# A fused attention and gated feed-forward kernel: its instruction order written out task by task, with a softmax chain in finer steps

## The chip, the cores and the metric

The kernel runs on one core of a Trainium2 chip. The metric is the device time of one execution in microseconds. In the profile, PE is the matrix engine and PEld its weight loads, DVE the vector engine, ACT the scalar engine, POOL the GpSimd engine and SP the engine that here only issues transfers. Times inside a profile count from the start of its span, which leaves out a little of the device time.

## The reference

Four batches of 6336 rows and 256 columns go through an attention over columns and then, row by row, through a gated layer.

```python
def _attn_ref(q, k, v, tau):                      # q, k, v: (4, 6336, 256)
    qn = q / (np.linalg.norm(q, axis=1, keepdims=True) + 1e-06)
    kn = k / (np.linalg.norm(k, axis=1, keepdims=True) + 1e-06)
    s = kn.transpose(0, 2, 1) @ qn / tau          # 256 x 256 in each batch
    s = s - s.max(-1, keepdims=True)
    a = np.exp(s)
    a /= a.sum(-1, keepdims=True) + 1e-09
    return (v @ a).astype(np.float32)

def _moe_ref(x, w_h, w_t, b_t):                   # x: (25344, 256)
    H = np.maximum(x @ w_h, 0.0)
    T = 1.0 / (1.0 + np.exp(-(x @ w_t + b_t)))
    return (T * H + (1.0 - T) * x).astype(np.float32)
```

## The kernel before

Each batch passes three parts.

- **Stage 1** reads q and k, 128 rows at a time (50 steps in a batch, called s), and sums the products of k with q, and of k and q with themselves for the norms, in two accumulators of the matrix engine.
- **The chain** turns the sums into the softmax matrix and folds the two weights into it (tiles mr0 and mr1).
- **Stage 2** takes 256 rows of v at a time (25 groups in a batch, 100 in all, called g): it transposes them (tr, and ev, the copy out), multiplies them by three matrices (h, t and x), applies relu (r) and gate (g) on ACT, and forms the product (p) and the result (y) on DVE. An output chunk is stored when its four groups are done.

Stage 1 of batch b+1 runs beside stage 2 of batch b. The stage 1 step, and the squares of q, which for the first 40 steps of batches 1 to 3 are taken from the matrix engine and given to ACT and POOL:

```python
for c in range(2):                                # in one step of stage 1
    nc.tensor.matmul(sg[c][:, 0:C], kc, qa, start=first, stop=False)
    nc.tensor.matmul(sg[c][:, C : C + P], kc, kc, start=False, stop=False)
    if not apart(b, s // CH):                     # b > 0 and chunk < 5
        nc.tensor.matmul(sg[c][:, C + P : C + 2 * P], qa[:, cs], qa[:, cs], ...)

def squares(b, j, half):                          # 128 x 1024 elements
    nc.scalar.activation(out=sq, in_=qa, func=Act.Square)

def sum_squares(b, j, step):                      # all on POOL
    if step == 0:   add(out=sq, in0=sq, in1=other)                       # 1024 wide
    elif step == 1: add(out=sq[:, 0:2, :], in0=sq[:, 0:2, :], in1=sq[:, 2:4, :])
    else:           ...                           # twice 256 wide
```

The chain, cut:

```python
dq = dve(lambda: (diagonal(0), diagonal(1), rest_of_q()), ...)   # norms of q
nq = pool(lambda: norm(0), ...)                   # square root
dk = dve(lambda: (diagonal(2), diagonal(3)), ...) # norms of k
nk = pool(lambda: norm(2), ...)
gs = act(copy_g, 0.58, 0.7, [dk], drop=own)       # both accumulators copied out
iq = dve(lambda: (recip(0), dcat()), ...)         # dcat: identity x 1/norm, 128 x 256
cqb = pe(bcast, 0.43, [iq], take=["vt"])          # ones @ dcat: 1/norm of q on all rows
# then scale, exp, transpose, copy, fold with the weights, and
def evac_ah(c, e):                                # 512 wide, one engine
    o, a, r = mr_t[b][c][:, C : 3 * C], st["ah", c], st["ri"][:, c : c + 1]
```

The order in which the instructions are emitted, which each engine then keeps, is chosen while the program is built. A small model of engines, buffers and transfers runs, and whenever an engine is free it takes the ready task with the lowest key:

```python
PRIO = {"tr": (24.974, 16.445, 34.195, 63.304), "ev": (74.59, ...), ...}

def pick(e):
    quiet = held(self.sums_stop)                  # no squares while a chain runs
    best = min((x for x in avail[e] if ready(x) and not (quiet and x.soft >= quiet)),
               key=lambda x: (x.key, x.n), default=None)
    lst = in_order.get(e)                         # loads and stores, in a fixed order
    if best is None and lst and ready(lst[-1]) and not (e == "POOL" and held(self.loads_stop)):
        return lst[-1]                            # no loads while a chain starts
    return best
```

Loads are issued by POOL and turn f32 into f16 on the way. Stores are issued by SP. To give loads the way, a store is put behind a later output tile by a small transfer called hold (held_row, 1 KB). In the last batch three and a quarter chunks of v are transposed by transfers (vT) and the rest by the matrix engine.

Of the kernel before, what the change touches and what calls it, by code (L numbers as in the profile page):

```python
# [15 lines left out]
P = 128  # L16
# [6 lines left out]
AHEAD = 16  # L23
BY_DMA = 3
SHORT = 1.08
MOVE = 165e3
APART = 5
V_AHEAD = 2


PRIO = {
    "tr": (24.974, 16.445, 34.195, 63.304),
    "ev": (74.59, 73.008, 67.512, 50.704),
    "h": (-53.39, -86.015, -64.208, -14.641),
    "bias": (-28.394, 23.065, -1.772, 4.453),
    "t": (4.111, -1.918, 67.766, 74.312),
    "relu": (46.555, -20.175, -1.498, 14.915),
    "x": (0.958, -19.433, 43.343, -6.4),
    "gate": (-54.132, 37.28, -94.231, -112.222),
    "prod": (-40.861, -10.819, -26.763, -55.482),  # L40
    "res": (53.604, 18.42, 116.457, -9.113),
    "s1": (117.419, 42.459, 84.45),
    "sq": (-15.195, 72.384, 19.395),
}
POW = 0.75
HEAD = 5.5
TAIL = 66
EV = BIAS = ("ACT", "DVE")
ENDS = [18, 48.5, 62.25]


class Ring:


    def __init__(self, bufs):
        self.bufs = bufs
        self.freed = []

    def open_at(self, t):
        n = len(self.freed) - self.bufs  # L60
        return n < 0 or (self.freed[n] is not None and self.freed[n] <= t)


class Task:
# [3 lines left out]

    def __init__(self, eng, key, pitch, lat, deps, fn, take=(), drop=(), size=0, follows=()):
        self.eng, self.key, self.pitch, self.lat = eng, key, pitch, lat
        self.deps, self.fn, self.take, self.drop, self.size = deps, fn, take, drop, size
        self.follows = follows
        self.start = self.done = None
        self.late = 0.0
        self.soft = 0
        self.held = {}
        self.serial = False

    def engines(self):
        return self.eng if isinstance(self.eng, tuple) else (self.eng,)

    def settle(self, e):
        n = self.eng.index(e)
        self.pitch, self.lat = self.pitch[n], self.lat[n]
        self.fn = partial(self.fn, e)
        self.eng = e


class Plan:

# [8 lines left out]
    def __init__(self):  # L101
        self.tasks = []
        self.rings = {}

        self.loads_stop, self.sums_stop = [], []

    def ring(self, tag, bufs):
        self.rings[tag] = Ring(bufs)

    def add(self, *args, **kw):  # L110
        t = Task(*args, **kw)
        self.tasks.append(t)
        return t

    def run(self):
        queues = {"POOL": [], "SP": []}
        in_order = {"POOL": [], "SP": []}
        users, followers = {}, {}
        for n, x in enumerate(self.tasks):
            x.n, x.left, x.at = n, len(x.deps) + len(x.follows), 0.0  # L120
            for d in x.deps:
                users.setdefault(d, []).append(x)
            for d in x.follows:
                followers.setdefault(d, []).append(x)
            if x.size or x.serial:
                in_order[x.eng].append(x)
        for lst in in_order.values():
            lst.sort(key=lambda x: (x.key, x.n), reverse=True)
        engines = list(dict.fromkeys(x.eng for x in self.tasks if not isinstance(x.eng, tuple)))
        avail = {e: [x for x in self.tasks if e in x.engines() and not x.left and not (x.size or x.serial)] for e in engines}  # L130
        free = dict.fromkeys(engines, 2.1)
        lanes, order, events = [], [], [0.0, 2.1]
        t, left = 0.0, len(self.tasks)
        eps = 1e-6

        def ready(x):
            return (
                not x.left
                and x.at <= t + eps
                and all(self.rings[g].open_at(t + eps) for g in x.take)  # L140
                and (x.eng != "POOL" or not x.size or sum(d > t + eps for d in lanes) < self.LANES)
            )

        def finish(x, when):
            x.done = when
            events.append(when)
            for owner, tag in x.drop:
                self.rings[tag].freed[owner.held[tag]] = when
            release(users.get(x, ()), when)

        def release(us, when):
            for u in us:
                u.left -= 1
                u.at = max(u.at, when)
                if not u.left and not (u.size or u.serial):
                    for e in u.engines():
                        avail[e].append(u)

        def pick(e):
            quiet = held(self.sums_stop)  # L160
            best = min(
                (x for x in avail[e] if ready(x) and not (quiet and x.soft >= quiet)),
                key=lambda x: (x.key, x.n), default=None,
            )
            lst = in_order.get(e)
            if best is None and lst and ready(lst[-1]) and not (e == "POOL" and held(self.loads_stop)):
                return lst[-1]
            return best

        def held(stops):  # L170
            return next(
                (
                    n + 1 for n, (a, b) in enumerate(stops)
                    if a.start is not None and (b.done is None or b.done > t + eps)
                ),
                0,
            )

        while left or any(queues.values()):
            for e in engines:  # L180
                x = pick(e) if free[e] <= t + eps else None
                if x is None:
                    continue
                if x.size or x.serial:
                    in_order[e].pop()
                else:
                    for other in x.engines():
                        avail[other].remove(x)
                    if isinstance(x.eng, tuple):
                        x.settle(e)  # L190
                left -= 1
                x.start = t
                order.append(x)
                for g in x.take:
                    x.held[g] = len(self.rings[g].freed)
                    self.rings[g].freed.append(None)
                free[e] = t + x.pitch
                release(followers.get(x, ()), free[e])
                events.append(max(free[e], t + 2 * eps))
                if x.size:  # L200
                    queues[e].append([x, float(x.size), t + self.HEAD])
                    events.append(t + self.HEAD)
                    if e == "POOL":
                        x.lane = len(lanes)
                        lanes.append(1e9)
                else:
                    finish(x, t + x.lat)

            act = [qq for qq in queues.values() if qq and qq[0][2] <= t + eps]
            share = self.RATE / max(1, len(act))  # L210
            nxt = [x for x in events if x > t + eps] + [t + qq[0][1] / share for qq in act]
            assert nxt, "no task can start"
            nxt = min(nxt)
            for qq in act:
                qq[0][1] -= share * (nxt - t)
            t = nxt
            events = [x for x in events if x > t - eps]
            for qq in act:
                if qq[0][1] < 1.0:
                    x = qq.pop(0)[0]  # L220
                    finish(x, t + self.LAG + x.late)
                    if x.eng == "POOL":
                        lanes[x.lane] = t + self.LAG
        self.end = max(x.done for x in order)
        return order
# [3 lines left out]
def kernel(  # L229
# [37 lines left out]
        "sq": 2, "vT": 3, "vT_t": 1, "o": O_BUFS, "ot": 1, "uu": 3, "pp": 3, "vtsb": 9, "mr0": 2, "mr1": 2,  # L267
        "sg0": 1, "sg1": 1, "vt": 1, "t": 1, "h": 2, "d": 2,
# [73 lines left out]
    def plan_load(nm, b, j, s=0, n=CH):  # L342

        size = P * n * C * 4 if j < NJ else TR * 2 * C * 4
        tag = nm if j < NJ else f"tail_{nm}"
        x = plan.add(
            "POOL", len(plan.tasks), 0.54, 0, [], lambda: load(nm, b, j, s, n),
            take=[tag] if s == 0 else [], size=size * (1 if j < NJ and n > 2 else SHORT),
        )
        ld.setdefault((nm, b, j), []).append(x)  # L350
        x.first = s
# [43 lines left out]
    plan_load("v", 0, 0)  # L395


    ends = [(-1, HEAD)] + [(e, (n + 1) * NS) for n, e in enumerate(ENDS)]

    def slot_of(n):  # L400

# [693 lines left out]
```

## Time and profile before

| what | value |
|---|---|
| device time, median of 3 runs | 270.34 us (270.19 to 270.39) |
| span of the profile | 268.3 us |
| PE, ACT, DVE, POOL busy | 246.4, 195.1, 181.6, 131.7 us |
| read from HBM, written to it | 78.38 MB, 25.95 MB |
| moved by the transfers, as received | 67.24 MB |

The profile page gives the busy time of each engine, the span in 40 slices, the chain of work that ended last and the costliest groups of instructions. In the page a matmul's end is modelled, so starts are the firmer reading. Transferred bytes count as they arrive: a load of f32 that lands as f16 counts half of what it reads.

### The profile page before, as it was taken

The numbers are of one execution on the slowest core, as the hardware profiler recorded it, in microseconds if no ns is written. First come the engines' busy times: TensorE is split into PE (matmuls) and PEld (weight loads), VectorE is DVE, ScalarE is ACT, GpSimd is POOL, SyncE is SP. The second block draws the span as 40 slices with busy tenths as digits, with TensorE's granted clock in tenths as the row PEclk, the third lists the DMA queues.
The fourth block names the chain that finished last, engine by engine and source line by source line (L and its number), as shares of the span: only waits on it lengthen the run. The fifth ranks groups of instructions, "written<-read, shape, count | busy, mean of one in ns | idle before, by whom it ended". The sixth has DMA issues, their size and how long they took to land.

```text
span 268.3 us, 6249 instructions
## 1 busy us (share of the span) xinstructions
PE 246.4 (92%) x2430; PEld 216.6 (81%) x2430; DVE 181.6 (68%) x377; ACT 195.1 (73%) x365; POOL 131.7 (49%) x167
## 2 busy tenths in 40 slices
PE   0697977999999999999999999999999999999991
PEld 0596864889989978999999878999998778888880
DVE  1000035777766789557878797586878998998994
ACT  1001016978888789999898887787798999998980
POOL 7233468688778064695689138567655110000000
PEclk9999999999999999999999999999999999999998
DMA  6999999999999999999999999999999999999995
GB/s 107 215 211 208 206 206 202 212 213 214 214 213 212 213 214 255 247 263 269 275 286 258 267 267 254 249 236 281 287 280 239 284 214 304 379 399 165 351 423 232
DMA packets 24622, 67.24 MB, mean 251 GB/s; under 512 B 9104, under 2 KB 11280, under 8 KB 21648
## 3 DMA queue, kind: packets, MB, share of 16 engines
q0 software_dynamic: 13472, 39.20, 75.0%
q1 hardware_dynamic: 11120, 27.64, 29.0%
q8 instruction: 19, 0.31, 0.4%
q14 instruction: 11, 0.09, 0.1%
HBM read 78.38 MB, written 25.95 MB: 389 GB/s over the span
## 4 chain that ended last, share of the span: by engine, by line
PE 76%; DMA 12%; ACT 5%; POOL 2%; issue 2%; DVE 2%; ACTq 0%; DVEq 0%; POOLq 0%
PE h L800 16%; PE t L800 16%; PE d L800 15%; PE sg L452 12%; DMA k<-in_k_dram 10%; PE sg L453 6%; PE vtps L760 5%; DMA v<-in_v_dram 2%; ACT uu L854 2%; PE sg L455 2%; PE t L831 1%; PE vtps L754 1%; PE ah L689 1%; POOL q L327 1%; ACT d L840 1%
## 5 line engine op out<-in xcount | busy, mean ns | idle before, releaser
L800 PEld LDWEIGHTS <-vtsb 128*128 128x128 f16 (+1 forms) x1044 | 98.8, 99 | 17.3 <-issue 3.2
L452 PE MATMUL sg<-q,k 128*128 128x256 f16 x384 | 83.8, 277 | 12.7 <-DMA k<-in_k_dram 12.6
L861 DVE SCALAR_TENSOR_TENSOR pp<-uu,d 128x512 f32<-128x512 f32 (+1 forms) x100 | 68.0, 684 | 28.4 <-PE d L800 16.1
L453 PE MATMUL sg<-k 128*128 128x128 f16 x384 | 76.8, 223 | 0.0
L854 ACT ACTIVATE uu<-t 128x512 f32<-128x512 f32 (+1 forms) x100 | 59.7, 597 | 19.1 <-PE t L800 18.5
L880 DVE SCALAR_TENSOR_TENSOR o<-h,pp 128x512 f32<-128x512 f32 x96 | 65.5, 686 | 1.7
L840 ACT ACTIVATE d<-h 128x512 f32<-128x512 f32 (+1 forms) x100 | 57.9, 584 | 5.7 <-PE h L800 4.9
L800 PE MATMUL t<-mr,vtsb 128*128 128x256 f16 (+1 forms) x348 | 52.2, 272 | 1.5 <-ACT t L533 1.2
L800 PE MATMUL h<-mr,vtsb 128*128 128x256 f16 (+1 forms) x348 | 51.2, 272 | 0.5 <-ACT vtsb L533 0.5
L800 PE MATMUL d<-mr,vtsb 128*128 128x256 f16 (+1 forms) x348 | 51.5, 272 | 0.1
L452 PEld LDWEIGHTS <-k 128*128 128x128 f16 x384 | 38.0, 99 | 16.7 <-DMA k<-in_k_dram 13.9
L476 POOL TENSOR_TENSOR sq<-sq,sq 128x1024 f32<-128x1024 f32 x15 | 35.4, 2361 | 16.7 <-ACT sq L470 16.6
L453 PEld LDWEIGHTS <-k 128*128 128x128 f16 x384 | 38.0, 99 | 1.5
L533 ACT COPY t<-bias_all 128x512 f32<-128x512 f32 (+1 forms) x60 | 35.4, 591 | 1.4
L455 PE MATMUL sg<-q 128*128 128x128 f16 x144 | 32.5, 226 | 0.0
L470 ACT ACTIVATE sq<-q 128x1024 f32<-128x1024 f16 x30 | 31.3, 1053 | 0.0
L760 PE MATMUL vtps<-ident,v 128*128 128x128 f32 x144 | 27.8, 275 | 0.9 <-DMA v<-in_v_dram 0.6
L569 DVE SCALAR_TENSOR_TENSOR junk<-sg,ident 128x128 f32<-128x128 f32 x16 | 4.6, 288 | 33.2 <-PE sg L455 32.7
L535 DVE COPY vtsb<-vtps 128x256 f32<-128x256 f32 (+2 forms) x47 | 19.6, 418 | 7.0 <-PE vtps L760 6.7
L327 POOL DMA_DIRECT2D v<-in_v_dram x24 | 13.7, 571 | 18.9 <-PE vtps L760 11.7
L327 POOL DMA_DIRECT2D q<-in_q_dram x28 | 15.4, 552 | 15.1 <-DMA q<-in_q_dram 7.1
L327 POOL DMA_DIRECT2D k<-in_k_dram x28 | 15.3, 548 | 13.1 <-DMA k<-in_k_dram 9.2
(78 smaller groups left out, 249.5 us busy)
## 6 DMA issues: line engine op xcount, KB each, us to landing
out_dram<-o SPq DMA_DIRECT2D x23, 1024.0 KB, 9.6
v<-in_v_dram POOLq DMA_DIRECT2D x24, 512.0 KB, 16.6
q<-in_q_dram POOLq DMA_DIRECT2D x21, 512.0 KB, 16.2
k<-in_k_dram POOLq DMA_DIRECT2D x21, 512.0 KB, 18.0
q<-in_q_dram POOLq DMA_DIRECT2D x5, 256.0 KB, 9.6
k<-in_k_dram POOLq DMA_DIRECT2D x5, 256.0 KB, 8.9
out_dram<-o SPq DMA_DIRECT2D x2, 512.0 KB, 4.2
out_dram<-ot SPq DMA_DIRECT2D x4, 192.0 KB, 5.1
```

Of the source, the lines that this page charges most:

```text
L327: nc.gpsimd.dma_start(out=t[:, s : s + n, :], in_=main_rows(src)[:, j * CH + s : j * CH + s + n, :])
L452: nc.tensor.matmul(sg[c][:, 0:C], kc, qa, start=first, stop=False)
L453: nc.tensor.matmul(sg[c][:, C : C + P], kc, kc, start=False, stop=False)
L455: nc.tensor.matmul(sg[c][:, C + P : C + 2 * P], qa[:, cs], qa[:, cs], start=False, stop=last)
L476: add(out=sq, in0=sq, in1=other)
L533: nc.scalar.copy(out=out, in_=in_)
L760: nc.tensor.transpose(ps[:, u, 0:nr], v.bitcast(f32), ident0[0:nr, 0:nr])
L800: nc.tensor.matmul(out[0:nr, u, :], vt[u][kt][:, 0:nr], mr[kt][:, col * C : (col + 1) * C], **flags(u, kt))
L840: nc.scalar.activation(out=d[0:nr, :, :], in_=ps_t["h", b, i][0:nr, :, :], func=Act.Relu, scale=0.5)
L854: nc.scalar.activation(out=uu[0:nr, :, :], in_=ps_t.pop(("t", b, i))[0:nr, :, :], func=Act.Tanh, scale=-0.5)
L861: nc.vector.scalar_tensor_tensor(out=pp[0:nr, :, :], in0=el.pop(("uu", b, i))[0:nr, :, :], scalar=1.0, in1=ps_t.pop(("d", b, i))[0:nr, :, ...
L880: nc.vector.scalar_tensor_tensor(out=ot, in0=ps_t.pop(("h", b, i))[0:nr, :, :], scalar=0.0, in1=el.pop(("pp", b, i))[0:nr, :, :], op0=AluO ...
```

## The change

The greedy choice and its keys are gone. A text lists every task in the order in which it is emitted, with its engine where two are possible, and the build only walks through it. Tasks that were bundles (both diagonals, both copies, both weights' halves) have names of their own, so that the list can place each.

```diff
-PRIO = { ... }
+ORDER = """
+Lk0.0 Lq0.0 const Lq0.1 Lk0.1 Lb1 Lk0.2 Lk0.6 Lb0 Lq0.6 Lq0.2 s0.0 s0.1 s0.2 s0.3 s0.4 s0.5 Lk0.3 s0.6 s0.7
... (cut)
+s0.27 s0.28 s0.29 Lk0.5.6 s0.30 s0.31 Lk1.0.0 s0.32 s0.33 s0.34 Lq1.0.0 s0.35 s0.36 s0.37 Lw1 s0.38 s0.39 Lw0
+s0.40 s0.41 Lv0.0 s0.42 s0.43 Lq1.0.4 s0.44 Lk1.0.4 s0.45 s0.46 s0.47 c0.dq0 c0.g1/ACT c0.g0/ACT c0.dq1 ball
+c0.dk0 c0.nq c0.dk1 c0.nk c0.iq sqq1.0.0/ACT c0.b Lq1.1 c0.ik s1.0 s1.1 Lk1.1 c0.s0 s1.2 c0.s1 Lv0.1 c0.e0
+Lq1.2 c0.e1 c0.tr0 Lk1.2 c0.v0/ACT c0.tr1 c0.r1 c0.f0 c0.r0 c0.v1/ACT Lv0.2 c0.a0 tr0 c0.t0/ACT c0.f1
+c0.h0/ACT ev0/DVE s1.3 b0/DVE c0.h1/ACT tr2 Lq1.3 c0.t1/ACT h0 c0.a1 ev2/ACT tr1 r0 t0 ev1/DVE x0 sqq1.0.1/DVE
... (cut)
+r94 t95 p93 g94 x94 b96/ACT y93 h95 p94 t96 r95 h96 g95 y94 x95 r96 O3.4.0 h97
+p95 g96 x96 y95 r97 t97 b98/ACT p96 h98 g97 x97 y96 r98 t98 p97 O3.5.0 h99 g98 x98 y97 r99 t99 p98 x99 g99 y98
+p99 O3.5.4 y99 O3.6
+"""
 class Plan:
     def run(self):
-        ... (the model of engines, buffers and transfers, and pick)
+        done = {id(x) for x in self.tasks.values() if x.fn is None}
+        for token in ORDER.split():
+            name, _, e = token.partition("/")
+            x = self.tasks[name]
+            assert all(id(d) in done for d in [*x.deps, *x.follows]), name
+            x.fn(e) if e else x.fn()
+            done.add(id(x))
```

In the names, L is a load, O a store, T a transfer that transposes, H a hold; s0.47 is step 47 of batch 0; c1.e0 is a step of batch 1's chain; the rest are the letters above with the group's number.

Squares are summed in one accumulator of 128x1024, and ACT or DVE may square:

```diff
-        nc.scalar.activation(out=sq, in_=qa, func=Act.Square)
+        if e == "ACT":
+            nc.scalar.activation(out=out, in_=x, func=Act.Square)
+        else:
+            (nc.vector if e == "DVE" else nc.gpsimd).tensor_tensor(out=out, in0=x, in1=x, op=AluOp.mult)
+    def add_square(nm, b, j, n, e):
+        eng, acc = nc.gpsimd if e == "POOL" else nc.vector, acc_t[nm, b]
+        eng.tensor_tensor(out=acc, in0=acc, in1=sq_t.pop((nm, b, j, n)), op=AluOp.add)
+    def fold_sums(nm, b, n, e): ...               # 512 and 256 wide, once in a batch
```

The chain loses the diagonal matrix: the inverse norms, repeated along the columns, become the weights of two matmuls with the identity. Copies that were 512 wide become two of 256:

```diff
-                nc.vector.tensor_scalar(out=st["dcat"][:, c, :], in0=ident0, ...)
-            nc.tensor.matmul(st["cqb"], ones, st["dcat"][:, :, :], start=True, stop=True)
+            for c in range(2):
+                nc.tensor.matmul(
+                    st["cqb"][:, c, :], st["inv"][:, c : c + 1].to_broadcast([P, P]), ident0,
+                    start=True, stop=True,
+                )
-        def evac_ah(c, e):
-            o, a, r = mr_t[b][c][:, C : 3 * C], st["ah", c], st["ri"][:, c : c + 1]
+        def evac_ah(c, n, e):
+            o = rows_of(c)[:, (n + 1) * C : (n + 2) * C]
+            a, r = st["ah", c][:, n * C : (n + 1) * C], st["ri"][:, c : c + 1]
```

Each of h, t and x now depends only on the copies that it reads. Two further forms of stage 2 (FORM_B, FORM_D) come with the change and are used by no group. The arithmetic of stage 1 and stage 2, the sizes and number of loads and stores, and the number of buffers stay the same.

## The prediction

> **What bounds the kernel now.** I read the page first: busy times, slices, HBM bytes and the chain of work that ended last.
>
> ```profile
> PE 246.4 (92%) x2430; PEld 216.6 (81%) x2430; DVE 181.6 (68%) x377; ACT 195.1 (73%) x365; POOL 131.7 (49%) x167
> ...
> PE   0697977999999999999999999999999999999991
> ...
> DMA  6999999999999999999999999999999999999995
> GB/s 107 215 211 208 206 206 202 212 213 214 214 213 212 213 214 255 247 263 269 275 286 258 267 267 254 249 236 281 287 280 239 284 214 304 379 399 165 351 423 232
> ...
> HBM read 78.38 MB, written 25.95 MB: 389 GB/s over the span
> ...
> PE 76%; DMA 12%; ACT 5%; POOL 2%; issue 2%; DVE 2%; ACTq 0%; DVEq 0%; POOLq 0%
> ```
>
> The matrix engine is full in nearly every slice after the sixth, and 76% of the chain is its own matmuls. But the transfer engines are just as full (the row DMA), from the first slice to the last. So there are two candidates, and each needs an account of its own.
>
> **The matrix engine's account.** Busy time misleads, because a matmul's reported end is modelled, so I take starts. In the timeline of the last groups one set of four matmuls starts 0.44 us after the other although each set lasts 0.60:
>
> ```profile
> 258.74 0.60 PE L800 MATMUL t<-mr,vT 128*128 128x256 f16 x4
> 259.18 0.60 PE L800 MATMUL h<-mr,vT 128*128 128x256 f16 x4
> ```
>
> Start to start, the timeline gives 0.109 us for a 256-wide matmul, 0.058 or 0.055 for a 128-wide f16 one, 0.109 for an f32 transpose, 0.216 for a 512-wide one. Times the counts of the page: stage 1 takes 400 x (0.109 + 0.058) + 160 x 0.055 = 75.6; h, t and x take 1200 x 0.109 = 130.8; transposes 150 x 0.109 + 48 x 0.056 = 19.1; bias rows, chain and the rest 12.8. The sum is 238.3, say **238 us of work**. The first matmul starts at 8.95 and the last ends at 262.64, with 5.7 us behind it to the end. So the gaps are 262.64 - 8.95 - 238 = **15.7 us**. Up to the first h, at 45.65, the work is 50 steps of stage 1 (22.2), 8 steps of batch 1 (2.7), chain, bias and transpose (2.7), 27.6 in all: gaps of 45.65 - 8.95 - 27.6 = 9.1. Later gaps are therefore only 6.6. The view of waits has few named ones:
>
> ```profile
> PE sg L452 <- DMA k<-in_k_dram: 12.6, 5, 9.0
> ...
> PE t L800 <- ACT t L533: 1.2, 3, 0.7
> ```
>
> The large one is the first data, 8.95 of it, which no order removes. Around the first h the timeline shows what else was waited for:
>
> ```profile
> 43.54 0.60 PE L689 MATMUL ah<-wht,et 128*128 128x512 f16 x2 [0.16 <-DVE et L535]
> 44.77 0.41 PE L760 MATMUL vtps<-ident,v 128*128 128x128 f32 x2 [0.63 <-DMA v<-in_v_dram]
> 45.65 0.61 PE L800 MATMUL h<-mr,vtsb 128*128 128x256 f16 x4 [0.46 <-ACT vtsb L533]
> ```
>
> The last weight fold of the chain is on its way at 43.54, then the engine waits for the first chunk of v, which lands at 44.7, and then for its transposed copy.
>
> **The transfers' account.** The view of stages (columns: PE, PEld, DVE, ACT, POOL busy, clock, DMA share, GB/s) has one stage with loads alone, one mixed, one with stores alone:
>
> ```profile
> 45.65:95.00 49.35, 49.09 (x488) 43.84 (x489) 34.65 (x61) 41.73 (x74) 33.48 (x38) 1.00 1.07 214
> 99.00:150.00 51.00, 51.00 (x511) 46.17 (x509) 39.03 (x74) 46.00 (x84) 35.78 (x41) 1.00 1.06 265
> 256.00:260.00 4.00, 4.00 (x38) 3.48 (x37) 3.69 (x7) 3.52 (x8) 0.00 (x0) 1.00 1.01 424
> ```
>
> Loads move 214 GB/s as received, stores 424. The queues of the page moved 39.20 MB of loads, hence 39.20/0.214 = 183.2 us; stores are 25.95/0.424 = 61.2 us; the 1.69 MB left of the stores' queue are the transposing transfers, which I put at the 165 GB/s of the slice around 245 us, where they move, 10.2 us. Together **254.6 us**. The first load starts to move at 8.95 - 2 x 2.45 = 4.05 (two chunks of 0.524 MB land before the first matmul), and the last store, issued at 264.60, lands 2.7 later, 1.05 before the end. So the floor of the transfers is 4.05 + 254.6 + 1.05 = **259.7 us**, and 268.3 - 259.7 = 8.6 us are lost. That is the tighter bound: the matrix engine without gaps would end at 8.95 + 238 + 5.7 = 252.7. One part of the loss can be seen. From 213 to 228 us, in 40 slices of 0.375 us, the rate falls away twice:
>
> ```profile
> GB/s 208 296 361 372 448 415 459 328 175 221 216 84 19 119 267 253 289 243 13 98 142 208 175 175 197 241 274 383 393 448 339 317 295 251 339 306 317 295 328 306
> ```
>
> Six slices lie between 13 and 142 GB/s, because loads of v wait for buffers and the stores are still held back: 2 to 3 us lost. The rest, some 5 to 6, is spread over small transfers at the start and over stretches where loads and stores mix.
>
> [...]the stage with both moves 265 GB/s, between the 214 and the 424. So order is all that the change can alter there. [...]
>
> **The change part by part.** *Squares.* ACT and POOL rows now:
>
> ```profile
> L476 POOL TENSOR_TENSOR sq<-sq,sq 128x1024 f32<-128x1024 f32 x15 | 35.4, 2361 | 16.7 <-ACT sq L470 16.6
> ...
> L470 ACT ACTIVATE sq<-q 128x1024 f32<-128x1024 f16 x30 | 31.3, 1053 | 0.0
> ```
>
> The list squares 16 times on ACT and 14 on DVE: ACT loses 14 x 1.053 = 14.7 us[...]. The list also moves 5 bias copies to ACT (+3.0) and with them 3 copies of transposes; ACT should end near 185, DVE near 195 (no diagonal matrices, -1.9; one add and four folds, +3.7; fewer copies, -4.6). POOL did adds of 35.4 + 19.2 + 8.8 + 8.8 + 2.2 = 74.4 us; now 26 of 2.361 and two folds, 63.4. None of the three becomes the bound over the whole span (70 to 74%), so this is room, worth nothing by itself.
>
> *Start.* In the list v's first chunk stands ahead of the second halves of batch 1's first q and k, which were ahead of it. Two halves of 0.262 MB at 214 GB/s are 2.45 us: v is there at 42.3, its copy near 43.2. The chain must be as early. It loses two 0.28 us operations for the diagonal, and its last copies, two of 0.751 one behind the other on DVE (ending at 44.93), become four halves, mostly on ACT, of about 0.38: I put its end at 43.4. First h at **43.4 instead of 45.65**. Fewer steps stand before it (4 of batch 1, two transposes: 26.4 instead of 27.6 of work), so the net is 2.25 - 1.2 = 1.0 us.
>
> *Middle and end.* Work left after h: 238 - 26.4 = 211.6. The later gaps of 6.6 lie mostly where a chain crosses the stream (95 to 99, 150 to 157, 205 to 218). With the single steps placed one by one and h, t and x released each by its own copies, I halve them: 3.3, a choice. The matrix engine then gives 43.4 + 211.6 + 3.3 + 5.7 = **264.0**.
>
> *Transfers.* The same bytes. In the list the stores of batch 2 begin well before the loads of the last v chunks, so that something is always queued; I give back 2.5 for the hole and 1 for the mixed stretches: 259.7 + 8.6 - 3.5 = **264.8**. The two accounts meet at 264.4. The device time stands 270.34 - 268.35 = 2.0 above the span: **266.4 us**.
>
> **The rivals.** *The transfers keep their losses.* For it: they are full in 99 to 150 without any gap in the matrix engine. Then shorter chains only lengthen the waits for data: 268 to 270. [...]Three of the 14 DVE squares stand in the list within 0.4 us of matrix work of an add on POOL[...]. DVE also frees the h banks, but it has a quarter of its time idle: 0 to 3 us more, 266 to 269. *A list too tight.* Many loads stand in it such that, at the rates above, they land within half a microsecond of their first use. A static list can't step aside, and every engine keeps its order. If real landings scatter, waits add up: 270 to 276. *A better list.* If both accounts lose half their gaps: 262 to 264. For it: such a list can be searched far more finely than a set of keys.
>
> **Range and chances.** The floors (252.7 and 259.7, plus 2.0) forbid much below 262, and the first two rivals end near 270. So 262.5 to 270.5. Faster by over 2% needs less than 264.9, 1.5 under my number: 0.37. Within 2%: 0.56. Slower by over 2% needs the third rival in full: 0.07.
>
> **What would show it.** First h near 43.4; gaps of the matrix engine after it near 3; no slices at 13 to 100 GB/s after 210; DVE busy near 195 and ACT near 185; last matmul near 258.3. I am wrong if waits for DMA appear at matmuls between 60 and 250, if DVE squares last 2 us or more, or if stores still trail by more than 6 us after the last matmul.

## The result, and the profile after

| | before | after |
|---|---|---|
| device time, median | 270.26 us | 285.54 us |
| ratio, with its 95% interval | | 1.056 (1.053 to 1.059) |
| span of the profile | 268.3 us | 283.2 us |
| last matmul ends | 262.6 us | 277.7 us |
| gaps of the matrix engine up to 45 us, and behind it | 8.5, 6.9 us | 9.2, 21.9 us |
| time the transfers lost | 9.9 us | 24.2 us |

The list made the kernel 5.6% slower. The gaps are worked out as in the prediction: for each matmul the time to the next start, less the usual pitch of its kind. The last row is the transfers' account kept at each landing: a full chunk loaded or stored is counted as 2.44 us (close to 0.524 MB at the measured 214 GB/s, or 1.05 MB at 424), smaller ones in proportion, and what the clock shows beyond the sum of all landed, counted from 4.04 us, is lost. Kept in this way it gives 9.9 us for the kernel before, where the prediction's sum gave 8.6. Both accounts lose about 15 us more than before. The work is nearly the same (8 matmuls more). Some executions are disturbed and take longer (524 us in one of e1's, 283 to 286 in the others), so each time is the median of the others, and of e1, f1, g1 and h3, whose profiled execution was disturbed, only times are used.

The page of the changed kernel, with the rows that the prediction used:

```profile
PE 249.2 (88%) x2438; PEld 219.1 (77%) x2438; DVE 199.8 (71%) x381; ACT 188.2 (66%) x366; POOL 121.2 (43%) x138
...
PE   0789969999979899979999889999973999999992
...
DMA  6999999999999999999999999969999958898994
...
PE 55%; DMA 27%; DVE 10%; issue 2%; ACT 2%; POOL 1%; SPq 1%; DVEq 0%; POOLq 0%; ACTq 0%
```

The transfers' row had nines from the second slice to the last but one; now it has a 6 at 184 to 191 us and falls off again from 226. The matrix engine's row breaks down to 7 and 3 at 205 to 219 us. In the chain that ended last, transfers rose from 12% to 27%. The stages say the same (columns: PE, PEld, DVE, ACT, POOL busy, clock, DMA share, GB/s), first before, then after:

```profile
185.00:205.00 20.00, 20.00 (x212) 18.34 (x209) 15.14 (x27) 17.27 (x31) 12.79 (x13) 1.00 1.07 264
205.00:225.00 20.00, 19.57 (x170) 15.99 (x170) 18.35 (x48) 18.40 (x41) 3.52 (x6) 1.00 1.03 258
```

```profile
185.00:205.00 20.00, 19.68 (x203) 17.69 (x202) 16.85 (x25) 15.90 (x30) 14.31 (x14) 1.00 0.84 165
205.00:225.00 20.00, 13.53 (x113) 11.26 (x112) 10.18 (x27) 7.71 (x15) 1.34 (x4) 0.83 1.04 343
```

Twenty microseconds in which the transfers move 165 instead of 264 GB/s come first, while the matrix engine still runs. Only then does the matrix engine stop, with the transfers full. So the hole at 210 us is a consequence. The timeline of DVE shows what it waited for; after the arrow stands what released it:

```profile
208.89 0.69 DVE L481 COPY t<-bias_all 128x512 f32<-128x512 f32 x1
216.37 0.69 DVE L861 SCALAR_TENSOR_TENSOR o<-h,pp 128x512 f32<-128x512 f32 x1 [6.79 <-DMA out_dram<-o]
```

A result waits for an output buffer, that is, for an old store to land. That store was issued only at 206.13 and landed at 216.29. The order of the queue that issues it is in SP's timeline, here of the changed kernel (held_row is a hold; x2 means two in one line, so the second hold of the second line ends at 190.03):

```profile
158.21 0.42 SPq L875 DMA_DIRECT2D out_dram<-o  x1
168.14 21.89 SPq L905 DMA_DIRECT2D held_row<-o  x2
190.08 0.57 SPq L875 DMA_DIRECT2D out_dram<-o  x1
199.66 0.50 SPq L905 DMA_DIRECT2D held_row<-o  x1
200.21 0.69 SPq L875 DMA_DIRECT2D out_dram<-o  x1
205.58 0.50 SPq L905 DMA_DIRECT2D held_row<-o  x1
206.13 1.13 SPq L875 DMA_DIRECT2D out_dram<-o  x2
```

And of the kernel before:

```profile
184.95 0.50 SPq L919 DMA_DIRECT2D held_row<-o  x1
185.50 0.58 SPq L894 DMA_DIRECT2D out_dram<-o  x1
193.49 0.50 SPq L919 DMA_DIRECT2D held_row<-o  x1
194.03 0.58 SPq L894 DMA_DIRECT2D out_dram<-o  x1
```

Before, each hold lets one store go, one every 8 to 9 us at this point. In the list the holds and stores are grouped: H11, then H13 and only O1.1, H14 and O1.2, H12, then five stores. H13 waits for a result that DVE writes from 188.80 to 189.49. No store is issued between 158.2 and 190.1 us, and from 206.1 on five go out one behind the other. POOL issues no load from 174.1 to 187.1 either; its additions wait for squares there:

```profile
174.07 0.55 POOL L259 DMA_DIRECT2D q<-in_q_dram  x1
181.33 5.78 POOL L401 TENSOR_TENSOR acc_q<-acc_q,sq_q 128x1024 f32<-128x1024 f32 x2 [6.71 <-ACT sq_q L395]
187.06 0.57 POOL L259 DMA_DIRECT2D k<-in_k_dram  x1
```

The last store issued lands at 180.17 and the last load at 187.08, so at 187 us both queues are empty.

A shorter wait of the same kind (2.0 us at 125) and a handful of others make up the rest. Three were candidates of their own: two squares on DVE that took 3.0 instead of 1.2 us, with matrix engine gaps of 0.83 and 1.65 us behind them; steps of the next batch that wait for diagonals of the chain (1.05 and 1.35 us); and loads behind additions on POOL.

### The profile page after: what moved, and what is told of

It reads as the page before. It is cut to its first block, busy times and chain, and to the rows that moved or that the text cites. A ratio compares the mean times of both kernels' runs of the same rounds, so it can differ in the third digit from the quotient of the medians.

```text
span 283.2 us, 6251 instructions
## 1 busy us (share of the span) xinstructions
PE 249.2 (88%) x2438; PEld 219.1 (77%) x2438; DVE 199.8 (71%) x381; ACT 188.2 (66%) x366; POOL 121.2 (43%) x138
## 4 chain that ended last, share of the span: by engine, by line
PE 55%; DMA 27%; DVE 10%; issue 2%; ACT 2%; POOL 1%; SPq 1%; DVEq 0%; POOLq 0%; ACTq 0%
DMA out_dram<-o 14%; PE h L728 12%; PE d L728 11%; PE t L728 11%; DMA q<-in_q_dram 11%; PE sg L370 7%; PE vtps L688 4%; PE sg L372 4%; DVE pp L815 3%; DVE o L861 3%; DMA held_row<-o 2%; DVE sq_q L397 2%; PE sg L374 1%; PE t L768 1%; PE vtps L682 1%
## 5 line engine op out<-in xcount | busy, mean ns | idle before, releaser
L370 PE MATMUL sg<-q,k 128*128 128x256 f16 x384 | 84.9, 276 | 13.1 <-DMA q<-in_q_dram 10.9
L401 POOL TENSOR_TENSOR acc_q<-acc_q,sq_q 128x1024 f32<-128x1024 f32 x26 | 62.5, 2405 | 51.5 <-DVE sq_q L397 24.8
L815 DVE SCALAR_TENSOR_TENSOR pp<-uu,d 128x512 f32<-128x512 f32 (+1 forms) x100 | 68.2, 682 | 15.0 <-PE d L728 10.5
L785 ACT ACTIVATE d<-h 128x512 f32<-128x512 f32 (+1 forms) x100 | 58.6, 586 | 26.3 <-PE h L728 23.9
L728 PE MATMUL h<-mr,vtsb 128*128 128x256 f16 (+1 forms) x348 | 52.4, 274 | 11.3 <-DVE o L861 10.7
L728 PE MATMUL d<-mr,vtsb 128*128 128x256 f16 (+1 forms) x348 | 52.6, 274 | 0.0
L479 ACT COPY t<-bias_all 128x512 f32<-128x512 f32 (+1 forms) x65 | 38.4, 591 | 1.1
L259 POOL DMA_DIRECT2D v<-in_v_dram x24 | 13.3, 554 | 35.6 <-PE vtps L688 25.5
L479 ACT COPY gs<-sg 128x256 f32<-128x256 f32 x8 | 2.9, 376 | 35.0 <-PE sg L374 35.0
L481 DVE COPY vtsb<-vtps 128x256 f32<-128x256 f32 (+2 forms) x44 | 18.2, 414 | 6.2 <-PE vtps L688 6.1
L397 DVE TENSOR_TENSOR sq_q<-q 128x1024 f32<-128x1024 f16 x14 | 20.8, 1488 | 0.0
L259 POOL DMA_DIRECT2D q<-in_q_dram x28 | 15.5, 555 | 10.6 <-DMA q<-in_q_dram 6.9
## 6 DMA issues: line engine op xcount, KB each, us to landing
v<-in_v_dram POOLq DMA_DIRECT2D x24, 512.0 KB, 10.2
k<-in_k_dram POOLq DMA_DIRECT2D x21, 512.0 KB, 11.4
k<-in_k_dram POOLq DMA_DIRECT2D x5, 256.0 KB, 11.4
q<-in_q_dram POOLq DMA_DIRECT2D x5, 256.0 KB, 12.1
```

The costliest lines, as they stand in the source:

```text
L259: nc.gpsimd.dma_start(out=t[:, s : s + n, :], in_=main_rows(src)[:, j * CH + s : j * CH + s + n, :])
L401: eng.tensor_tensor(out=acc, in0=acc, in1=sq_t.pop((nm, b, j, n)), op=AluOp.add)
L479: nc.scalar.copy(out=out, in_=in_)
L728: nc.tensor.matmul(out[0:nr, u, :], vt[u][kt][:, 0:nr], mr[kt][:, col * C : (col + 1) * C], **flags(u, kt))
L785: nc.scalar.activation(out=d[0:nr, :, :], in_=h[0:nr, :, :], func=Act.Relu, scale=scale)
L815: nc.vector.scalar_tensor_tensor(out=pp[0:nr, :, :], in0=el.pop(("uu", b, i))[0:nr, :, :], scalar=1.0, in1=d[0:nr, :, :], op0=AluOp.add, o ...
```

## The experiments

Beside these runs the kernel before stood at 270.1 to 270.4 us.

| run | kernel | us | ratio to before (95%) |
|---|---|---|---|
| e1 | after, a row for each hold | 284.6 | 1.050 (1.042 to 1.058) |
| e2 | after, 14 squares to ACT | 289.5 | 1.069 (1.063 to 1.075) |
| e3 | after, eight output buffers | 278.0 | 1.026 (1.022 to 1.031) |
| e4 | before, with the new chain | 274.5 | 1.015 (1.009 to 1.022) |
| f1 | before, eight output buffers | 270.4 | 1.002 (1.001 to 1.004) |
| f2 | after, eight buffers and eight rows | 274.9 | 1.018 (1.013 to 1.023) |
| f3 | f2, loads ahead of additions | 279.0 | 1.034 (1.027 to 1.041) |
| f4 | f3, two squares to ACT | 281.6 | 1.042 (1.037 to 1.047) |
| g1 | f2, two squares moved | 275.5 | 1.019 (1.017 to 1.021) |
| g2 | f2, chain operations moved | 274.2 | 1.015 (1.013 to 1.017) |
| g3 | f2, both moved | 273.5 | 1.013 (1.011 to 1.015) |
| g4 | f2, no holds | 282.4 | 1.045 (1.043 to 1.048) |
| h1 | after, SP nearly in the old order | 279.2 | 1.033 (1.027 to 1.038) |
| h2 | g3, SP nearly in the old order | 276.4 | 1.022 (1.014 to 1.029) |
| h3 | before, SP in the list's order | 296.0 | 1.093 (1.088 to 1.098) |
| k1 | after, SP in the old order | 273.4 | 1.012 (1.008 to 1.015) |
| k2 | g3, SP in the old order | 271.2 | 1.004 (1.002 to 1.007) |

### Single suspects

**e1.** All holds write one row, so a hold also waits for the one before it to land (47.8 us in 11 waits of SP in the changed kernel). Theory B is that the squares on DVE cost the time.

```diff
-    held_row = const.tile([1, C], f32, tag="held_row")
     def hold(b, j):
+        held_row = const.tile([1, C], f32, tag=f"held_row{b}_{j}", name=...)
```

> The changed kernel, with a row of its own for every hold, so that no hold waits for the one before it to land. Theory A (the written list is too tight: it leaves no time for waits that its timetable didn't have, the largest of them the 6.6 us at 210 us, where a result waits for an output buffer whose store stands behind two holds that wait for each other): the stall at 210 us shrinks to under 2 us and the slow clock after it goes too, so 276 to 280 us instead of 285.5. Theory B [...]: 284 us or more. Theory C (transfers lose rate by the new mix): 284 us or more.

1 us came back by the medians, and that is not clear of the spread (282.9 to 285.9, against 285.0 to 285.7 for the changed kernel). The holds' wait for each other is not the main cause.

**e2.** The squares of DVE at the same places of the list, on ACT.

```diff
-... sqq1.0.1/DVE ... sqq1.1.0/DVE ...          (14 of them)
+... sqq1.0.1/ACT ... sqq1.1.0/ACT ...
```

> The changed kernel, its 14 squares on DVE given to ACT at the same places of the list. Theory B [...]: the two squares of 3.0 us and the matrix engine's waits of 1.5 and 0.7 us behind them go, and if this is the main cause the time falls to 272 to 277 us. Theory A: the stall at 210 us stays, ACT gets 15 us more work, 282 to 287 us.

4 us worse: ACT, in its fixed order, is now late with biases (the matrix engine waits 3.9 us for them), and the wait for an output buffer stays, 6.8 us. So taking the squares off DVE brings nothing back here. As ACT is late in turn, this run alone does not clear them; k1 below does, with all 14 left on DVE.

**e3.** One more output buffer.

```diff
-O_BUFS = 7
+O_BUFS = 8
```

> The changed kernel with eight output buffers instead of seven, the list as it is. Theory A: both waits of a result for a landing store (2.1 us near 125 us and 6.8 us near 210 us) go, with the slow clock after the second: 275 to 278 us. Theory B: 284 us or more. If the store falls back by more than one chunk, a part of the wait stays: 279 to 282 us.

As expected for the buffers: 7.5 us came back and the large wait is gone. But the transfers still lose 17.3 us, and the stores now trail 10.6 us behind the last matmul. The buffer was where the trouble showed; something still makes the stores late.

**f1.** The control: the same edit in the kernel before.

> The kernel before with eight output buffers in place of seven. It separates two readings of what the eighth buffer did for the changed kernel. Theory A (the changed list spends its output buffers faster than its stores give them back; the order before does not): no wait for an output buffer of any size in the kernel before, so 269.5 to 271 us. Rival (any order of this program gains from an eighth buffer): 263 to 267 us.

Nothing gained. Seven buffers were enough for the old order; it is the list that runs out.

**f2.** Both edits together, with eight rows used in turn (eight rows fit beside the extra buffer).

```diff
+    held_rows = [const.tile([1, C], f32, tag=f"held_row{i}", ...) for i in range(8)]
-        nc.sync.dma_start(out=held_row, in_=og[(b, j)][0:1, 0, :])
+        nc.sync.dma_start(out=held_rows[(b * NJ + j) % 8], in_=og[(b, j)][0:1, 0, :])
```

> The changed kernel with eight output buffers and eight rows for the held marks in turn, so that a mark does not wait for the one before it to land. Theory A (the stores fall behind on SP because the marks stand one behind the other): the tail of stores behind the last matmul shrinks from 10.6 us to 7 or 8, the time is 274.5 to 277 us. Rival (a mark is waited for because of its row's result, not of the one before): as with eight buffers alone, 277 to 279 us.

274.9 (275.2 in the expectations of the g runs, which count one more execution), with the last stores 7.4 us behind the last matmul instead of 10.6. With a buffer to spare, the holds' wait for each other counts for 3 us more.

### The chain by itself

**e4.** The kernel before, greedy order kept, with the chain's new operations in it.

```diff
-        iq = dve(lambda: (recip(0), dcat()), ...)
-            nc.tensor.matmul(st["cqb"], ones, st["dcat"][:, :, :], start=True, stop=True)
+        iq = dve(lambda: recip(0), ...)
+            for c in range(2):
+                nc.tensor.matmul(st["cqb"][:, c * P : (c + 1) * P],
+                    st["inv"][:, c : c + 1].to_broadcast([P, P]), ident0, start=True, stop=True)
         def evac_ah(c, e):                       # half on ACT, half on DVE
```

> The kernel before, greedy order kept as it was, with two parts of the new chain alone: no diagonal matrix (the inverse norms as weights against the identity) and the last copies in two halves, one on ACT and one on DVE. Theory A: these parts are harmless and worth little, 269 to 270.5 us. Theory D (the new chain itself is slow, by its matmuls with repeated columns as weights): 272 us or more.

4 us slower: in theory D's range, but not by its mechanism, since four matmuls with repeated columns take 0.44 to 0.52 us from their start to the next one in the changed kernel, and the two that they replace took 0.43 to 0.49 before. The gaps of the matrix engine grow from 15.4 to 18.9 us, and one new one, at 164.2 us, has 2.25 of the 3.5. DVE's timeline, and POOL's:

```profile
163.13 2.93 DVE L655 TENSOR_SCALAR mr<-e,ri 128x256 f16<-128x256 f32 x1
```

```profile
163.53 2.36 POOL L476 TENSOR_TENSOR sq<-sq,sq 128x1024 f32<-128x1024 f32 x1
```

The same operation takes 0.35 us on average in the kernel before. There it had run at 162.00, just ahead of POOL's next load (162.10) and addition (162.64); the shifted chain puts it just behind the issue of a load (162.99), which the addition follows until 165.89, and it ends with that addition. This one clash accounts for 2.25 of the 3.5 us of added gaps; the rest was not separated. A part that is shorter by itself can lose more by where it falls.

### The squares, the chain's places, the loads

**f3.** 54 loads moved in the list ahead of POOL's additions, where their buffers allow.

```diff
-... L.. behind adq../POOL ...                   (54 loads)
+... L.. ahead of adq../POOL ...
```

> As f2, with 54 of the loads moved in the list ahead of the additions of GpSimd that they stood behind, as far as their buffers are free by then. Theory A (transfers stand idle because loads are issued late behind additions that wait for squares): no stretch without a load issued between 171 and 184 us, 4 to 7 us less of lost transfer time, 269 to 273 us. Rival (the transfers catch up by themselves, or a load that now waits for its buffer holds up GpSimd and the squares): 274 to 279 us.

4 us worse than f2, and the transfers still fall to 193 GB/s from 185 to 205 us (202 in f2). POOL, too, keeps its order: now additions stand behind loads that wait for their buffers, the squares' buffers come free late, and DVE and ACT are late in turn. The rival's half of the expectation held. Loads behind additions are not what has to be mended, at least not this way.

**f4.** On f3, the two long squares on ACT.

```diff
-sqq1.1.1/DVE ... sqq1.4.1/DVE
+sqq1.1.1/ACT ... sqq1.4.1/ACT
```

> As f3, with the two squares of VectorE that took 3.0 us instead of 1.2 beside an addition given to ScalarE. Theory A [...]: 1 to 2.5 us less than f3. Rival (the transfers set the pace there, the matrix engine's gap is made up): within 0.7 us of f3, or worse where ScalarE is late in its turn.

Worse again: one of them waits 4.25 us on ACT for a buffer that an addition still reads, and the bias behind it holds up the matrix engine for 5.0 us. This says little of the squares beside additions, as f3's order caused that wait.

**g1, g2, g3.** On f2, by hand.

```diff
 g1, g3:
-sqq1.1.0/DVE r2 Lk1.3 t2 x2 Lv0.3 g2 y1 s1.8 adq1.1.0/POOL ev3/ACT s1.9 sqq1.1.1/DVE
+sqq1.1.0/DVE sqq1.1.1/DVE r2 Lk1.3 t2 x2 Lv0.3 g2 y1 s1.8 adq1.1.0/POOL ev3/ACT s1.9
+and sqq1.4.1/DVE ahead of p11
 g2, g3:
+c1.dk1 behind c1.dq0, c2.dq1 behind c2.dq0, adq2.0.1/POOL behind c1.ik
```

> The changed kernel with eight output buffers and eight rows for the marks (275.2 us), and the two VectorE squares that took 3.0 us moved one or two places forward[...]. Theory A ([...]each 3.0 us square cost the matrix engine 0.8 and 1.6 us): no square over 2 us at 51 and 75 us, both gaps of the matrix engine gone, 273 to 274 us. Rival (the matrix engine makes such gaps up while it waits for transfers later): 274.8 to 275.6 us.

> The same base (275.2 us), with one diagonal of the chain of batch 1 and one of batch 2 moved forward in VectorE's order, ahead of the product and the result they stood behind, and one addition of GpSimd moved behind the chain's small operations. Theory A (the steps of the next batch wait for these diagonals, 1.05 and 1.35 us[...]): these three gaps shrink to under 0.3 us each, 272 to 273.5 us. Rival (made up later while transfers are waited for): 274.8 to 275.6 us.

> Both sets of moves on the same base. Theory A (the lost time after 45 us is a sum of single places where an engine's fixed order waits): 270 to 271.5 us, level with the kernel before, whose order was not touched by hand. Rival (once one place is mended another takes over, since all later landings and starts shift): 272.5 to 276 us.

g1 gains nothing that can be seen (275.5 against 274.9). In g3 the two squares there are back at 1.2 us, as POOL is now the later one (in k2, with the same moves, its additions there take 3.20 and 2.96 us instead of 2.36), yet the gaps behind them are 1.33 and 1.13 us, in sum what they were (0.83 and 1.65): two squares in a row make DVE's results late as well. g2 removes gaps of 3.1 us less the 1.5 that stay, and gains 0.7 (273.7 to 275.3, against 274.8 to 275.6 for f2, so not clear of the spread). g3 gains 1.4 (273.3 to 274.1). So in these lists a gap mended is repaid in part only, and the transfers keep losing 13.3 us.

**g4.** f2 without holds.

```diff
-UNTIL = 73                                      (and the 13 H in the list)
+UNTIL = -1
```

> The same base (275.2 us) without the 13 marks that hold the stores back, so that a store is issued as soon as its chunk is done. Theory A (the marks buy early loads and are needed: stores would go between the loads from 60 us on): loads land later from 60 us on, gaps for q, k or v at the matrix engine, 277 to 285 us. Rival (the marks only delay the stores in this list): 271 to 275 us, a shorter tail.

7.5 us worse, as theory A had it; the matrix engine waits again from 75 us on. The stores must be held back. The question is only how.

### The order of holds and stores

**h1, k1.** The changed kernel as it is (seven buffers, one row), with SP's own order put back: each hold stands behind the first result of its chunk, and the store five chunks older behind the hold.

```diff
-H5 H6 O0.0.0 O0.1.0 H7 O0.2.0 H9 O0.3.0 H10 O0.4.0 O1.0.0 O0.6 O0.5.0 H11 H13 O1.1.0 H14 O1.2.0
-H12 O1.3.0 O2.0.0 O1.6 O1.4.0 O1.5.0 H8 O2.3.0 H15 H16 O2.2.0 T3.3 ...       (SP's part of the list)
+H5 O0.0.0 O0.6 H6 O0.1.0 H7 O0.2.0 H8 O0.3.0 H9 O0.4.0 H10 O0.5.0 H11 O1.0.0 O1.6 H12 O1.1.0
+H13 O1.2.0 H14 O1.3.0 H15 O1.4.0 H16 O1.5.0 T3.3 H17 O2.0.0 O2.1.0 ...       (k1; in h1 T3.3 is behind O2.5.0)
```

> The changed kernel with seven output buffers and one row for the marks, as it was; only SP's order is that of the kernel before: behind the first result of a chunk its mark and the one store that belongs to it. Theory A (the grouping of marks and stores starves the transfer engines at 185 to 200 us and later fills them at once, so that buffers come free late): no stretch without a store between 155 and 186 us, no wait of 6 us for an output buffer, the lost transfer time falls from 24 to 12 to 15 us, 272 to 277 us. Rival (the loads behind GpSimd's additions and the lateness of every engine cause it, the stores only show it): 280 to 286 us.

h1 gains 6.3 us, and has no wait for an output buffer left. What remained was my own slip: I had put the transposing transfer T3.3 behind six stores, and the matrix engine waits for it:

```profile
246.83 0.38 PE L765 MATMUL t<-btb,row 128*128 128x512 f16 x1
251.65 0.93 PE L725 MATMUL t<-mr,vT 128*128 128x256 f16 x4 [4.44 <-DMA vT<-v]
```

> h1 with the transposing transfers in their old places too, so that all of SP's instructions stand in the order of the kernel before and nothing else of the change is undone. Theory A (SP's order is the largest part of the loss): the wait of 4.6 us at 247 us goes, 273.5 to 276 us, some 10 us of the 15. Rival (the wait moves on to another load or buffer): 277 to 280 us.

With T3.3 in its old place, **273.4 us: 12.1 of the 15.3 us are back from SP's order alone.** The stages of k1:

```profile
185.00:205.00 20.00, 20.00 (x207) 17.92 (x206) 18.06 (x28) 15.17 (x28) 11.59 (x12) 1.00 1.01 225
205.00:225.00 20.00, 20.00 (x185) 17.30 (x183) 18.50 (x49) 17.81 (x39) 2.48 (x4) 1.00 1.07 251
```

The matrix engine is full in both, and the clock too. POOL still issues no load from 171.3 to 184.3 us, as in the changed kernel, but now stores are issued within that stretch. SP's timeline of k1, stores alone:

```profile
164.69 0.58 SPq L872 DMA_DIRECT2D out_dram<-o  x1
...
176.83 0.33 SPq L870 DMA_DIRECT2D out_dram<-ot  x1
...
179.11 0.58 SPq L872 DMA_DIRECT2D out_dram<-o  x1
...
187.28 0.58 SPq L872 DMA_DIRECT2D out_dram<-o  x1
```

The store at 179.11 is O1.1, which the list let go at 190.08.

**h2, k2.** The same two orders on g3.

> The changed kernel with the stores in the order of before, eight output buffers, eight rows for the marks, the two squares and the chain's operations moved (273.5 us without the stores' order). Theory A: the 3.4 us of transfer time that it loses beyond the kernel before come back, 268.5 to 271.5 us. Rival (loads are the cause): 272.5 to 275 us.

> h2 with the same mend: SP's order of before, eight output buffers, eight rows, the two squares and the chain's operations moved. Theory A: 270 to 272.5 us, level with the kernel before and with a transfer loss of 10 to 12 us. Rival (the wait moves on): 274 to 276.5 us.

h2 waits 3.2 us for T3.3 and is behind g3. k2 comes to 271.2 us, 0.4% behind the kernel before. The lost time of the transfers up to a moment:

| us lost by | 160 | 180 | 200 | 220 | 240 | end | later gaps of PE |
|---|---|---|---|---|---|---|---|
| before | 4.9 | 5.6 | 6.6 | 6.4 | 8.7 | 9.9 | 6.9 |
| after | 5.2 | 8.8 | 10.5 | 14.3 | 17.6 | 24.2 | 21.9 |
| f2 | 5.7 | 4.6 | 8.2 | 12.1 | 11.8 | 14.7 | 10.2 |
| k1 | 4.7 | 4.5 | 5.7 | 8.7 | 11.4 | 13.2 | 10.0 |
| k2 | 5.5 | 4.5 | 6.9 | 6.6 | 9.7 | 10.5 | 7.6 |

Up to 160 us all five are alike; what differs arises behind that, and k2 ends next to before in both accounts.

**h3.** The converse, on the kernel before with its scheduler.

```diff
+    for n, name in enumerate(STORES.split()):    # the list's order of H, O and T
+        sp_tasks[name].key = n
```

> The kernel before, scheduler and all, with marks and stores in the order of the list on SP; the scheduler shifts other work a little to fit. Theory A (that order by itself makes transfers idle and buffers late): 276 to 284 us. Rival (only together with the list's loads and squares): 269.5 to 273 us.

9.3% slower, more than expected. The list's order of holds and stores is harmful without the rest of the list too. The scheduler also shifts other work to fit, so the size is not that of the stores' order alone.

## Why the prediction was wrong

Point by point, by its own steps:

- **What bounds the kernel: right.** The matrix engine's work and the bytes are nearly what they were; the two accounts of losses, 31.1 us of gaps and 24.2 us of transfers, explain the time.
- **Start: right in kind, two thirds in size.** v's first chunk landed at 42.0 (42.3 predicted), the first h started at 44.13 instead of 45.65, where 43.4 was predicted. It did not shorten the run.
- **Squares and busy times: about right.** DVE ended at 199.8 (195), ACT at 188.2 (185). The 14 squares on DVE took 20.8 us, one alone 1.216; what the prediction counted for one was its author's estimate. DVE's rows of before, 0.288 us for 128 columns and 0.686 for 512, extended to 1024 give an estimate of 1.22.
- **Middle and end of the matrix engine: wrong.** "I halve them: 3.3, a choice." They came to 21.9. Of the 15.0 more than the 6.9 before, the one wait at 210 us is 6.5, and the half clock behind it 2.4.
- **Transfers: the step that failed.** "In the list the stores of batch 2 begin well before the loads of the last v chunks, so that something is always queued; I give back 2.5 for the hole and 1 for the mixed stretches". In place of 3.5 us given back, 14.3 more were lost. I read where the names of stores stand in the list, not what stands before them on SP: a hold waits for a result, and everything behind it waits too. H11 and H13 in front of O1.1 kept SP without a store from 158 to 190 us, and H14 and H12 put off O1.3, whose buffer the result at 210 us needed, to 206.13. k1 shows that this order is 12.1 of the 15.3 us: with the old one the transfers lose 13.2 us instead of 24.2.
- **The rivals.** "A list too tight" pointed the right way, with a range (270 to 276) that ends 9.5 us short and too small a chance, and it had another mechanism: not loads that land half a microsecond late, but a queue whose order leaves the transfers idle and the buffers full. Two squares on DVE beside an addition on POOL did take longer (3.07 and 3.02 us), and one addition beside a square (3.34 instead of 2.36); moving the two squares gained nothing by itself (g1), and k1, which has 12.1 us back, has all 14 at their places in the list.

Of the 3.0 us between k1 and before, buffers, rows and the moved operations give 2.2 (k2). What the last 0.8 us are was not separated.

## What to carry to other kernels

When an order is written out, write down for each in-order queue what every entry waits for, and check the longest stretch without a transfer: holds and the stores they release belong in pairs, one by one. A wait for a buffer in the middle of a kernel can be the end of a story that began where the transfers ran empty, here some 20 us earlier; look for the first slice of the transfers that is not full. And judge a hand-made order only as a whole: moves aimed at a visible gap gained little or nothing (g1, g2) or made it worse (e2, f3).

## What the runs showed of the hardware

**Behind a pause of 6.5 us the matrix engine ran at half its clock.** In the changed kernel the gap ends at 217.1 us:

```profile
217.11 1.01 PE L728 MATMUL h<-mr,vtsb 128*128 128x256 f16 x4 [6.47 <-DVE o L861]
```

Four matmuls take 0.85 us from start to start in what follows, against 0.44; the granted clock is 0.50 until 221.9 us, so that some 2.4 us of work are lost on top of the 6.5. In h1 the same follows the 4.4 us wait: 0.50 from 252 us, and until some 255. But the clock was lower elsewhere too: 0.50 from 40.5 to 47.3 us in f3, and 0.96 in the mean up to 45 us in g3, where the longest wait of the chain's matmuls is 2.1 us. The changed kernel has the same wait and a clock of 1.00 up to 45 us. What decides is not shown.

**A square on DVE and an addition on POOL drew each other out.** After, DVE, then POOL:

```profile
51.08 3.07 DVE L397 TENSOR_TENSOR sq_q<-q 128x1024 f32<-128x1024 f16 x1
```

```profile
50.71 2.36 POOL L401 TENSOR_TENSOR acc_q<-acc_q,sq_q 128x1024 f32<-128x1024 f32 x1 [0.18 <-DVE sq_q L397]
```

The square started 0.37 us into the addition and took about as long as the rest of it and a square's own 1.22 us: 1.99 + 1.22 = 3.21, measured 3.07. Where an addition started second, it was the longer one (in k2, 3.20 us from 50.77, with a pair of squares on DVE from 49.26 to 51.76). Not expected was how small an operation can be drawn out: the scaling of 256 columns took 2.93 us in e4, against 0.35, beside an addition, and in f3 one on two columns, inv, took 2.64 us, against 0.16 on average in the kernel before. The scaling ended with the addition, but had started 0.40 us ahead of its recorded start, while POOL was issuing a load. Whether these two have the cause of the long squares is not shown, nor what that cause is.

**A hold is small, but does not land fast.** Its 1 KB took 6.0 us in the middle to land (4.1 to 27.0, in g3; 4.9 in the changed kernel, 1.6 to 16.8).
